# A second fold of the feature transform, with even and odd frequencies apart, and squares added on VectorE ahead of the norm's products

## The chip, the cores and the metric

The kernel runs on one core of a Trainium2 chip. The metric is device time in microseconds (us) of one execution; lower is better. The engines of the core that appear below are TensorE (PE; its weight loads are listed apart as PEld), VectorE (DVE), ScalarE (ACT), GpSimd (POOL) and SyncE (SP), which issues most DMA transfers. Every engine works through its own queue in order, and semaphores make an instruction wait for work of another engine.

## What is computed

The inputs are float32: q, k, v of shape (4, 8, 1152, 64) and two weight matrices, 512x2048 and 2048x512. The reference, cut to what matters:

```python
q_pool = q.reshape(B, H, S // 2, 2, D).mean(axis=3)          # 576 queries of 1152
scores = np.matmul(q_pool, k.transpose(0, 1, 3, 2)) / np.sqrt(D)
attn = softmax(scores)
x = np.matmul(attn, v)              # then heads side by side: x is (4, 576, 512)

X = np.fft.fft(np.fft.fft(x, axis=1), axis=2)
u = x + np.real(X)
un = (u - mean(u)) / np.sqrt(var(u) + 1e-06)                 # over the 512 features
ch = np.maximum(un @ w_ch1, 0.0) @ w_ch2
out = u + ch
```

The real part of the two-dimensional transform is cos over features times cos over tokens, less sin times sin. Below it is called the DFT, the mean and variance the norm, and the two products with w_ch1 and w_ch2 the FFN.

## The kernel before

**Attention.** Work goes by units: a unit is a pair of heads and one block of 128 queries, 5 units to a pair, 80 in all. In a unit TensorE makes the scores (L209, two float32r products to a piece of 384 keys), VectorE takes them out of PSUM with a running minimum (L211), ScalarE takes the exponential (L223), TensorE transposes (L236), ScalarE and in one case of five VectorE copy the transposed tiles to SBUF (L239), and TensorE multiplies with v (L252). When a batch's 8 heads are done, its x stands in two tiles, `ua` and `ub`, [128, 2, 576] each, with features on partitions.

**The middle of a batch** (`mid`: `dft`, then `norm`). `ub` holds features 256 to 511 in mirrored order (the heads' order HEADS, and the mirrored columns of v, see to most of that), so that feature n of `ua` lies beside 512-n of `ub`; a few one-row copies (L418 to L424) put right the rows that don't fit. Then sums and differences `xs` (L431) fold the features once, L445 folds the tokens, and the transform over features is a product with a contraction over 256 features, two tiles of 128 (L454): 256 sine columns, 258 cosine columns. A product with a contraction over a single row (L452, constant `alt`) brings in feature 256. The token transform is L462. `norm` sums the features with a product with `onesm` (L494), subtracts the mean, squares on ScalarE (L503), sums the squares with 24 products of one column each (L510, an [128, 96] block of squares as weights each time), and spreads 1/sqrt(var) with L527.

**What a float32 product is.** In the trace each float32 product of these stages stands as two matmul instructions with a weight load each: the 24 products of L510 are 48.

**FFN.** A block is 12 products of 288 columns (L615 to L617, three to a tile). The first layer's block ends with a Relu on ScalarE (L633) and a remainder on VectorE (L634), the second's with an addition on VectorE (L645). There are 64 blocks to a batch.

**What sets the order.** One program text emits all of it, in an order that a planner writes out: it keeps a clock `now`, adds the cost each step yields, and lets `mid` steps run when they are due and FFN blocks when TensorE credit has come up. A step of `mid` yields (TensorE cost, delay until the next step may be emitted); `gap` is 600 ns for the first three batches and 0 for the last one. The engines then run what they were given in that order, whatever time it really takes. Batch 3's `mid` runs after the last attention unit, beside the remaining FFN blocks of batch 2. Conversions of the weights (L559 to L577, on ScalarE, VectorE and GpSimd) run beside the attention of batches 0 to 2.

## Time and profile before

| | |
|---|---|
| time, median of 3 runs | 1076.02 us (1073.26 to 1076.13) |
| profiled execution, span of its instructions | 1075.9 us |
| TensorE matmul busy | 1015.1 us, 94% |
| TensorE weight load busy | 935.1 us, 87% |
| VectorE busy | 597.9 us, 56% |
| ScalarE busy | 529.4 us, 49% |
| GpSimd busy | 366.1 us, 34% |
| mean granted TensorE clock | 0.974 |

The profile shows no total of the profiled execution apart from its span; the span lies 0.1 us under the median of the runs. The busy share is an average over stages with different limits. Matmuls overlap one another in the records, so the time that a row of matmuls takes is read from the start of the first to the start of what follows. The granted clock is the share of TensorE's full speed (2.4 GHz) that it was given; 0.5 is its lower level, 1.2 GHz.

### The profile page before, as it was taken

To read this page: it belongs to the slowest core of one execution; us is meant where nothing else is said; L and a number is where in the kernel's file an instruction comes from. 1 tells how busy PE (TensorE), PEld (TensorE's weight loads), DVE (VectorE), ACT (ScalarE), POOL (GpSimd) and SP (SyncE) were. 2 spreads that over 40 slices of the span, in tenths; PEclk is the share of its full clock that TensorE was granted. 3 is DMA by queue.
4 is the path that set the end of the run, shared out by engine and by line. 5 is a ranking of instruction groups with operands and counts; after the bars stand their busy time and mean duration, and the time that the engine had idled before them with its cause. 6 is when DMAs were issued, how large, how long until landed. Compare 5 with 4: busy or idle time off the path is not lost.

```text
span 1075.9 us, 22038 instructions
## 1 busy us (share of the span) xinstructions
PE 1015.1 (94%) x8688; PEld 935.1 (87%) x8688; DVE 597.9 (56%) x1542; ACT 529.4 (49%) x1045; POOL 366.1 (34%) x351
## 2 busy tenths in 40 slices
PE   6999998998999989996699999999999999999998
PEld 5898887687999876896599998789999997999998
DVE  5556868877575676665535455654464433442222
ACT  5778876677565665464245454454454431221111
POOL 3545665757455556435322222320220002000000
PEclk9999999989999999998799999999999999899999
DMA  5545644655667653745634433333533242356554
GB/s 181 178 133 173 201 155 166 194 160 186 201 216 245 217 175 106 226 139 182 210 99 165 148 130 118 98 109 131 163 106 113 79 141 70 115 173 198 163 166 153
DMA packets 53709, 168.97 MB, mean 157 GB/s; under 512 B 8083, under 2 KB 11300, under 8 KB 53606
## 3 DMA queue, kind: packets, MB, share of 16 engines
q1 hardware_dynamic: 49286, 149.87, 43.2%
q0 software_dynamic: 4320, 17.70, 5.1%
q8 instruction: 68, 1.11, 0.4%
q14 instruction: 35, 0.29, 0.1%
HBM read 145.97 MB, written 21.57 MB: 156 GB/s over the span
## 4 chain that ended last, share of the span: by engine, by line
PE 70%; DVE 8%; issue 3%; POOL 3%; DMA 2%; ACT 2%; SPq 0%; DVEq 0%; POOLq 0%; ACTq 0%
PE s L209 9%; PE o L252 9%; PE f L615 9%; PE f L616 8%; PE f L617 8%; PE t L236 8%; PE t L615 4%; PE t L617 4%; PE t L616 4%; DVE sp L211 2%; PE f L462 2%; PE f L510 1%; PE f L454 1%; DMA w<-wraw 1%; ACT sp L223 1%
## 5 line engine op out<-in xcount | busy, mean ns | idle before, releaser
L211 DVE TENSOR_SCALAR_CACHE_REDUCE sp<-s,bia 128x384 f32<-128x384 f32 x288 | 177.4, 616 | 98.0 <-PE s L209 77.6
L209 PE MATMUL s<-ks,qh 128*128 128x384 f32 x480 | 185.2, 386 | 26.0 <-DVE sp L211 8.6
L239 ACT COPY pt<-t 128x512 f32<-128x512 f32 (+2 forms) x243 | 126.0, 529 | 126.4 <-PE t L236 122.5
L223 ACT ACTIVATE sp<-sp,bia 128x1152 f32<-128x1152 f32 x144 | 180.0, 1255 | 1.8 <-DVE sp L211 1.7
L252 PE MATMUL o<-pt,vs 128*64 128x128 f32 (+1 forms) x2880 | 167.7, 269 | 3.4 <-DVE pt L239 2.9
L252 PEld LDWEIGHTS o<-pt,vs 128*64 128x64 f32 x2880 | 147.8, 139 | 24.9 <-issue 19.0
L209 PE MATMUL s<-ks,ql 128*128 128x384 f32 x480 | 165.5, 345 | 0.0
L236 PE MATMUL t<-ident,sp 128*128 128x128 f32 x1045 | 152.5, 278 | 1.7 <-ACT sp L223 0.7
L236 PEld LDWEIGHTS t<-ident,sp 128*128 128x128 f32 x1045 | 124.6, 142 | 13.8 <-issue 4.1
L209 PEld LDWEIGHTS s<-ks,qh 128*128 128x128 f32 x480 | 93.1, 194 | 34.0 <-DVE sp L211 11.4
L615 PE MATMUL f<-unh,w 128*128 128x288 f32 x348 | 107.5, 309 | 5.0 <-DVE g L634 5.0
L615 PE MATMUL f<-g,w 128*128 128x288 f32 x348 | 108.0, 310 | 3.1 <-DVE x L645 1.4
L616 PE MATMUL f<-unh,w 128*128 128x288 f32 x348 | 103.9, 299 | 0.0
L617 PE MATMUL f<-unl,w 128*128 128x288 f32 x348 | 103.7, 298 | 0.0
L616 PE MATMUL f<-g,w 128*128 128x288 f32 x348 | 103.7, 298 | 0.0
L617 PE MATMUL f<-g,w 128*128 128x288 f32 x348 | 103.5, 297 | 0.0
L634 DVE SCALAR_TENSOR_TENSOR g<-f,g 128x288 fp32r<-128x288 f32 x87 | 39.7, 457 | 106.7 <-ACT g L633 106.5
L645 DVE TENSOR_TENSOR x<-f,x 128x288 f32<-128x288 f32 x87 | 39.7, 456 | 104.2 <-PE f L617 104.2
L209 PEld LDWEIGHTS s<-ks,ql 128*128 128x128 f32 x480 | 93.5, 195 | 0.6 <-POOL ql L158 0.4
L179 POOL TENSOR_TENSOR ks<-kr,ks 64x1152 fp32r<-64x1152 f32 x30 | 80.6, 2685 | 32.8 <-issue 16.5
L575 POOL TENSOR_TENSOR rest<-rest,wt 128x512 f32<-128x512 f32 x32 | 42.4, 1326 | 143.0 <-DVE wt L570 97.8
L633 ACT ACTIVATE g<-f 128x288 fp32r<-128x288 f32 x87 | 35.4, 410 | 103.5 <-PE f L617 103.4
(129 smaller groups left out, 2015.5 us busy)
## 6 DMA issues: line engine op xcount, KB each, us to landing
w<-w SPq DMA_DIRECT2D x128, 512.0 KB
qr<-in_q SPq DMA_DIRECT2D x30, 576.0 KB
ks<-in_k POOLq DMA_DIRECT2D x30, 576.0 KB, 5.6
wraw<-in_w SPq DMA_DIRECT2D x32, 512.0 KB
w<-wraw SPq DMA_DIRECT2D x32, 512.0 KB
vs<-in_v SPq DMA_DIRECT2D x32, 288.0 KB
kr<-in_k SPq DMA_DIRECT2D x30, 288.0 KB
out<-x SPq DMA_DIRECT2D x12, 288.0 KB
```

The costliest lines, as they stand in the source:

```text
L179: nc.gpsimd.tensor_tensor(ks[D:, :], kr[D:, :], ks[D:, :].bitcast(F32), op=ALU.subtract)
L209: nc.tensor.matmul(ps, lhsT=l, rhs=k, start=i == 0, stop=i == len(ops) - 1)
L211: nc.vector.tensor_scalar(sp[n, j][:, c], ps, -0.0625, bt[:, pc - 1:pc] if pc else None, op0=ALU.mult, op1=ALU.min, accum_out=bt[:, pc:pc ...
L223: last_exp[0] = nc.scalar.activation(t, t, AF.Exp, bias=bia.pop((n, j))[:, 2:3], scale=-1.0, accum_out=den[pr][:, col:col + 1]).ins
L236: nc.tensor.transpose(ps[:, i * P:i * P + P], sp[k][:, c * P:(c + 1) * P], ident)
L239: (nc.vector.tensor_copy if eng == "v" else nc.scalar.copy)(pt[:, :o], ps[:, :o])
L252: nc.tensor.matmul(po[y * D:y * D + D, :w], lhsT=qkv[2 * pr + y][3][:, c, :], rhs=pt[:, o:o + w], start=c == 0, stop=c == NKC - 1)
L575: nc.gpsimd.tensor_tensor(rest, rest, t[:, 0, :], op=ALU.mult)
L615: nc.tensor.matmul(ps, lhsT=ah, rhs=bh, start=first, stop=False)
L616: nc.tensor.matmul(ps, lhsT=al, rhs=bh, start=False, stop=False)
L617: nc.tensor.matmul(ps, lhsT=ah, rhs=bl, start=False, stop=last)
L634: after(1000, lambda: nc.vector.scalar_tensor_tensor(g[:, 1, c], ps[:, :HT], 0.0, g[:, 0, c].bitcast(F32), op0=ALU.max, op1=ALU.subtract))
```

## The change

The DFT folds the features a second time: feature n lies beside 256-n as well. The rows of the two tiles are ordered for that on the host (UROW, HEADS, MIRRORED). After the fold, even frequencies need a+c or a-c, odd ones the other, so that each product has one contraction over 128 rows and half as many frequencies: per block of 96 or 97 tokens two products of 128 columns (sine), or three of 65, 64 and 128 columns (cosine), in place of two of 256, or one single-row product and two of 258. The constant `alt` goes. VectorE and ScalarE get the second fold (`fold`) and other one-row copies, in smaller pieces with a planner's delay between them. In `norm`, VectorE adds the four blocks of squares to one, and 6 products are left of 24. The costs that `dft` and `norm` tell the planner are halved where products are (900 to 450, 2000 to 1000).

```diff
-        nc.vector.tensor_copy(tmp[D:D + 1], ub[:1])
-        nc.scalar.copy(last, ub[D:D + 1, 1, :])
+        nc.vector.tensor_copy(tmp[D:D + 1, 0, :], ua[:1, 1, :])
+        nc.scalar.copy(last, ub[:1, 1, :])
         yield 0, gap
-        nc.vector.tensor_copy(ub[:1, 1, :], ub[D:D + 1, 0, :])
+        nc.vector.tensor_copy(tmp[D:D + 1, 1, :], ub[:1, 0, :])
+        nc.scalar.copy(ua[:1, 1, :], ua[D:D + 1, 1, :])
+        yield 0, gap
         nc.vector.tensor_copy(ub[:1, 0, :], last)
-        yield 0, 1500
-        nc.scalar.copy(ub[D:D + 1], tmp[D:D + 1])
-        yield 0, 1800
+        nc.scalar.copy(ub[:1, 1, :], ub[D:D + 1, 0, :])
+        yield 0, gap
+        nc.vector.tensor_copy(ua[D:D + 1, 1, :], tmp[D:D + 1, 0, :])
+        yield 0, gap
+        nc.scalar.copy(ub[D:D + 1, 0, :], tmp[D:D + 1, 1, :])
+        yield 0, 1200
...
+        def fold(y):
...
+            for j in range(2):
+                nc.vector.tensor_tensor(e[:, j, 1:HT], e[:, j, 1:HT], e[:, j, NH:], op=ops[y])
+                yield 0, gap
+            if y:
+                nc.vector.tensor_tensor(o, a, c, op=ALU.subtract)
+                yield 0, gap
+                nc.vector.tensor_tensor(a, a, c, op=ALU.add)
+                yield 0, gap
+                nc.vector.tensor_copy(a[:1], c[:1])
+                sets.extend(((a, SSETS[0], slice(0, P)), (o, SSETS[1], slice(P, 2 * P))))
+                yield 0, 2500 if gap else 4500
+            else:
+                nc.vector.tensor_tensor(o, a, c, op=ALU.subtract)
+                yield 0, gap
+                nc.vector.tensor_tensor(c, a, c, op=ALU.add)
+                yield 0, gap
+                nc.scalar.copy(a, c)
+                yield 0, 800
+                nc.vector.tensor_copy(c[:1], o[:1])
+                nc.scalar.copy(o[:1], z)
+                sets.extend(((a, CSETS[0], slice(0, 65)), (c, CSETS[1], slice(65, 129)), (o, CSETS[2], slice(129, 257))))
+                yield 0, 1500
...
-                if y == 0:
-                    nc.tensor.matmul(ps[:m, :n], lhsT=z[:, c], rhs=alt, start=True, stop=False)
-                for j in range(2):
-                    nc.tensor.matmul(ps[:m, :n], lhsT=e[:, j, c], rhs=c1[:, j, :], start=y == 1 and j == 0, stop=j == 1)
+                for e, o, i in sets:
+                    nc.tensor.matmul(ps[:m, o], lhsT=e[:, c], rhs=c1[:, 0, i], start=True, stop=True)
                 nc.scalar.copy(yy[:m, t, :], ps[:m, :n])
-                yield 900, 0 if t < 2 else 1200 if y or not gap else 3000
+                yield 450, 0 if t < 2 else 1200 if y or not gap else 3000
...
+        for sq in sqs:
+            nc.vector.tensor_tensor(sq[:, :2], sq[:, :2], sq[:, 2:], op=ALU.add)
+            yield 0, gap
+            nc.vector.tensor_tensor(sq[:, 0], sq[:, 0], sq[:, 1], op=ALU.add)
+            yield 0, 900
         ps = gtile()
         for t, sq in enumerate(sqs):
             for i in range(3):
-                for j in range(4):
-                    nc.tensor.matmul(ps[:96, 3 * t + i:3 * t + i + 1], lhsT=sq[:, j, i * 96:i * 96 + 96], rhs=onesm[:, :1],
-                                     start=j == 0, stop=j == 3)
-        yield 2000, 0
+                nc.tensor.matmul(ps[:96, 3 * t + i:3 * t + i + 1], lhsT=sq[:, 0, i * 96:i * 96 + 96], rhs=onesm[:, :1],
+                                 start=True, stop=True)
+        yield 1000, 0
```

The order of the instructions moves in three places that matter here. The line numbers of the changed kernel are its own: its L423 to L434 are the one-row copies, L441 the first fold, L456 to L474 the token fold and the second feature fold, L488 the transform over features, L541 and L543 the additions of squares, L548 the sum of squares; L672 is before's L634, L683 before's L645, L292 before's L287.

VectorE, batch 3's `mid` after the last attention unit. Before:

```order
L634 SCALAR_TENSOR_TENSOR g<-f,g 128x288 [waits Activation_49] x2
L418 COPY tmp<-x 1x1152 [waits DVE_49,Pool_49]
L421 COPY x<-x 1x576 [waits DVE_49]
L422 COPY x<-last 1x576 [waits Activation_49]
L634 SCALAR_TENSOR_TENSOR g<-t,g 128x288 [waits Activation_49]
L645 TENSOR_TENSOR x<-t,x 128x288 [waits PE_49] x2
L431 TENSOR_TENSOR xs_10630<-x 128x576 [waits DVE_49,Activation_49]
L431 TENSOR_TENSOR xs_10630<-x 128x576
L431 TENSOR_TENSOR xs_10633<-x 128x576 x2
```

The same place in the changed kernel (z is a one-row sum, xs_10581 the differences, xs_10584 the sums):

```order
L672 SCALAR_TENSOR_TENSOR g<-t,g 128x288 [waits Activation_49]
L441 TENSOR_TENSOR xs_10581<-x 128x576 [waits DVE_49] x2
L441 TENSOR_TENSOR xs_10584<-x 128x576 x2
L447 TENSOR_TENSOR z<-xs_10581 1x287 [waits DVE_49]
L448 COPY z<-xs_10581 1x2
L456 TENSOR_TENSOR xs_10581<-xs_10581 128x287 [waits DVE_49]
L456 TENSOR_TENSOR xs_10581<-xs_10581 128x287
L459 TENSOR_TENSOR bs<-xs_10581 128x289 [waits DVE_49]
L461 TENSOR_TENSOR xs_10581<-xs_10581 128x289 [waits DVE_49]
L463 COPY xs_10581<-xs_10581 1x289 [waits DVE_49]
L672 SCALAR_TENSOR_TENSOR g<-t,g 128x288 [waits Activation_49]
L683 TENSOR_TENSOR x<-t,x 128x288 [waits PE_49] x3
```

There are eight remainders (L634, then L672) after the last attention unit in each kernel. Before, the eighth stands ahead of the first fold; in the changed kernel it stands behind the first fold, the token fold and the second fold of the differences.

TensorE, the same batch: the end of the FFN block ahead of the sine transform, the transform, and the block behind it. Before, two FFN blocks more stand ahead of it:

```order
L615 MATMUL f<-g,w_10600 128x288
L616 MATMUL f<-g,w_10600 128x288
L617 MATMUL f<-g,w_10600 128x288
L454 MATMUL f<-cs_109,xs_10633 97x256 [waits DVE_49] x2
L454 MATMUL t<-cs_109,xs_10633 96x256 x4
```

In the changed kernel:

```order
L653 MATMUL t<-g,w_10518 128x288 [waits Activation_49]
L654 MATMUL t<-g,w_10518 128x288
L655 MATMUL t<-g,w_10518 128x288 [waits DVE_49]
L488 MATMUL t<-cs_109,xs_10581 97x128
L488 MATMUL t<-cs_109,bs 97x128
L488 MATMUL f<-cs_109,xs_10581 96x128
L488 MATMUL f<-cs_109,bs 96x128
```

Between the transpose of the reciprocals (L265, the last product of the attention) and the sine transform there are 13 FFN blocks before, 8 of the first layer and 5 of the second. There are 11 in the changed kernel: one of the second layer, 8 of the first, 2 of the second. The wait of L655 is for the eighth L672.

TensorE, the sum of squares of batch 3. Before:

```order
L510 MATMUL t<-onesm,sq 96x1 x12
L510 MATMUL t<-onesm,sq 96x1 [waits Activation_49]
L510 MATMUL t<-onesm,sq 96x1 x11
```

In the changed kernel:

```order
L548 MATMUL t<-onesm,sq 96x1 [waits DVE_49,PE_49]
L548 MATMUL t<-onesm,sq 96x1 x2
L548 MATMUL t<-onesm,sq 96x1 [waits DVE_49]
L548 MATMUL t<-onesm,sq 96x1 x2
```

It waits for VectorE where it waited for ScalarE. In batch 0 the longer chain of delays also moves the first FFN block: before, it stands behind the 32nd unit's product with v, in the changed kernel behind the 34th's. At the 50th unit both kernels emit all that is left of batch 0's FFN, since a tile of x is needed again.

## Rows read from the trace of the kernel before

**Rows 1.** The page, part 1: engine, busy us, share of the span, instructions.

```profile
PE 1015.1 (94%) x8688; PEld 935.1 (87%) x8688; DVE 597.9 (56%) x1542; ACT 529.4 (49%) x1045; POOL 366.1 (34%) x351
```

**Rows 2.** The page, part 4: shares of the chain that ended last, by engine.

```profile
PE 70%; DVE 8%; issue 3%; POOL 3%; DMA 2%; ACT 2%; SPq 0%; DVEq 0%; POOLq 0%; ACTq 0%
```

**Rows 3.** Windows (stretch, busy us by engine, PEclk, DMA) over batches 0, 1, 2.

```profile
160.00:260.00 100.00, 90.67 (x774) 75.00 (x772) 84.11 (x195) 68.69 (x132) 61.88 (x56) 0.95 0.50 164
360.00:460.00 100.00, 89.15 (x744) 76.63 (x743) 69.96 (x164) 59.14 (x114) 59.85 (x54) 0.97 0.54 170
640.00:720.00 80.00, 77.20 (x649) 67.42 (x646) 48.19 (x123) 39.72 (x76) 25.98 (x28) 0.98 0.36 111
```

**Rows 4.** Timeline (start, us, what) of TensorE, batch 3: FFN, transforms, sum of squares.

```profile
882.11 0.30 PE L615 MATMUL t<-g,w 128*128 128x288 f32 x1
...
890.05 1.02 PE L454 MATMUL f<-cs,xs 128*97 128x256 f32 x4
...
892.45 0.48 PE L615 MATMUL t<-g,w 128*128 128x288 f32 x1
...
898.84 0.67 PE L452 MATMUL f<-alt,bs 1*97 1x258 f32 x2
...
903.49 0.48 PE L615 MATMUL t<-g,w 128*128 128x288 f32 x1
...
925.47 5.61 PE L510 MATMUL t<-onesm,sq 128*96 128x1 f32 x48
930.94 0.59 PE L615 MATMUL t<-g,w 128*128 128x288 f32 x1
```

**Rows 5.** Windows around that sum of squares; the clock follows POOL.

```profile
926.00:928.00 2.00, 2.00 (x25) 2.00 (x25) 0.13 (x1) 0.00 (x0) 0.00 (x0) 0.97 0.31 125
928.00:930.00 2.00, 2.00 (x15) 2.00 (x14) 0.00 (x0) 0.00 (x0) 0.00 (x0) 0.50 0.00 0
...
934.00:936.00 2.00, 2.00 (x14) 2.00 (x14) 0.46 (x1) 0.00 (x0) 0.00 (x0) 0.83 0.34 92
```

**Rows 6.** Timeline of TensorE: ten 128-column transposes at full clock.

```profile
461.66 1.25 PE L236 MATMUL t<-ident,sp 128*128 128x128 f32 x10
462.67 0.38 PE L615 MATMUL f<-g,w 128*128 128x288 f32 x1
```

**Rows 7.** Groups by line on VectorE: busy, mean ns of one | idle before.

```profile
L431 DVE TENSOR_TENSOR xs<-x 128x576 f32<-128x576 f32 x16 | 16.0, 1023 | 0.0
L445 DVE TENSOR_TENSOR xs<-xs 128x287 f32<-128x287 f32 x16 | 8.3, 530 | 0.0
L485 DVE TENSOR_TENSOR lsum<-x 128x576 f32<-128x576 f32 x8 | 9.2, 1160 | 0.0
```

**Rows 8.** Timeline, batch 0: first fold on VectorE, GpSimd beside it.

```profile
170.17 4.76 DVE L431 TENSOR_TENSOR xs<-x 128x576 f32<-128x576 f32 x2
...
171.26 3.05 POOL L179 TENSOR_TENSOR ks<-kr,ks 64x1152 fp32r<-64x1152 f32 x1
```

**Rows 9.** Timeline of VectorE, batch 3 after the last attention unit.

```profile
878.32 0.75 DVE L287 TENSOR_TENSOR x<-x,r 128x576 f32<-128x576 f32 x1
...
881.15 0.46 DVE L634 SCALAR_TENSOR_TENSOR g<-f,g 128x288 fp32r<-128x288 f32 x1 [1.14 <-ACT g L633]
...
882.42 0.45 DVE L421 COPY x<-x 1x576 f32<-1x576 f32 x1
...
883.28 0.44 DVE L634 SCALAR_TENSOR_TENSOR g<-t,g 128x288 fp32r<-128x288 f32 x1
...
885.86 2.75 DVE L431 TENSOR_TENSOR xs<-x 128x576 f32<-128x576 f32 x4
...
888.97 0.81 DVE L445 TENSOR_TENSOR xs<-xs 128x287 f32<-128x287 f32 x2
```

**Rows 10.** TensorE behind a stall: its timeline, and a window behind it.

```profile
500.53 0.61 PE L615 MATMUL f<-unh,w 128*128 128x288 f32 x1 [4.97 <-DVE g L634]
...
502.00:504.00 2.00, 2.00 (x10) 2.00 (x9) 1.82 (x5) 0.49 (x1) 0.00 (x0) 0.50 0.62 197
```

More of the change, by code (lines that the diff above doesn't have):

```diff
@@ L432, in dft @@
                 yield 0, gap
-            xs.append(e)
+            xs.insert(0, e)
         bs = mtile([P, 3, NH], F32, "bs")
-        z = bs[:1, 2, :]
-        nc.vector.tensor_tensor(z[:, 1:HT], last[:, 1:HT], last[:, NH:], op=ALU.add)
-        nc.vector.tensor_copy(z[:, 0:NH:HT], last[:, 0:NH:HT])
-        for y, n in ((1, 256), (0, 258)):
+        x1 = xs[1][:1, 0, :]
+        nc.vector.tensor_tensor(z[:, 1:HT], x1[:, 1:HT], x1[:, NH:], op=ALU.add)
+        nc.vector.tensor_copy(z[:, 0:NH:HT], x1[:, 0:NH:HT])
+        def fold(y):
+            e = xs[y]
+            ops = ALU.add, ALU.subtract
+            a, c, o = e[:, 0, :NH], e[:, 1, :NH], bs[:, 2, :]
+            for j in range(2):
[20 more added lines that the diff above has]
+                yield 0, 1500
+        for y, n in ((1, 256), (0, 257)):
             c1, c2 = ((cc1, cc2), (cs1, cs2))[y]
-            e = xs[y]
-            for j in range(2):
-                nc.vector.tensor_tensor(e[:, j, 1:HT], e[:, j, 1:HT], e[:, j, NH:], op=(ALU.add, ALU.subtract)[y])
-                yield 0, gap if j == 0 else 1500 if y == 0 else 2500 if gap else 4500
+            sets = []
+            yield from fold(y)
             yy = mtile([97, 3, n], F32, f"y{y}")
@@ L450, in dft @@
                 c = slice(t0, t0 + m)
-                if y == 0:
-                    nc.tensor.matmul(ps[:m, :n], lhsT=z[:, c], rhs=alt, start=True, stop=False)
-                for j in range(2):
-                    nc.tensor.matmul(ps[:m, :n], lhsT=e[:, j, c], rhs=c1[:, j, :], start=y == 1 and j == 0, stop=j == 1)
+                for e, o, i in sets:
+                    nc.tensor.matmul(ps[:m, o], lhsT=e[:, c], rhs=c1[:, 0, i], start=True, stop=True)
                 nc.scalar.copy(yy[:m, t, :], ps[:m, :n])
-                yield 900, 0 if t < 2 else 1200 if y or not gap else 3000
+                yield 450, 0 if t < 2 else 1200 if y or not gap else 3000
             for j in range(3 - y):
@@ L780, in _constants @@
 def _constants():
-    n = np.arange(DM // 2)
-    a1 = 2 * np.pi * (np.outer(n, np.arange(257)) % DM) / DM
+    a1 = 2 * np.pi * (np.outer(np.arange(P), FREQ) % DM) / DM
+    c1 = np.cos(a1)
+    s1 = np.sin(a1)
+    s1[0] = np.sin(np.pi / 2 * (FREQ % 4))
+    s1[0, ::2] = 0.0
     n1 = np.arange(NH)
     a2 = 2 * np.pi * (np.outer(n1, n1) % SQ) / SQ
-    c1 = np.zeros((DM // 2, 258))
-    c1[:, :257] = np.cos(a1)
-    s1 = np.sin(a1[:, :256])
-    s1[:, 0] = 0.0
+    c1 = np.concatenate([c1[:, x] for x in CSETS], axis=1)
+    s1 = np.concatenate([s1[:, x] for x in SSETS], axis=1)
     c2 = np.cos(a2)
@@ L795, in _constants @@
     for i, m in enumerate((c1, s1)):
-        t = m.reshape(2, P, -1).transpose(1, 0, 2).reshape(P, -1)
-        out[i, :, :t.shape[1]] = t
+        out[i, :, :m.shape[1]] = m
     for i, m in enumerate((c2, s2)):
@@ L804, in _constants @@
     out[4, :, P:2 * P] = 1.0 / DM
-    out[4, 0, 2 * P + 1:2 * P + 257:2] = -2.0
     return out
@@ L817 @@
     vt = v.copy()
-    vt[:, H // 2:] = v[:, H // 2:][..., VCOL]
+    vt[:, MIRRORED] = v[:, MIRRORED][..., VCOL]
     v2 = vt.reshape(B, H, NKC, P, D).transpose(0, 1, 3, 2, 4)
```

17 lines of the change are left out of this document (10 added, 7 removed).

## The prediction

> **What bounds the kernel now.** I read the engines' shares first: TensorE is busy 94% of the span, no other engine over 56% [rows 1], and the chain that ended last runs through TensorE for 70% and through VectorE for 8% [rows 2]. So time taken off TensorE counts wherever TensorE is what others wait for. The windows over the middle of each batch show how far that holds there. In 160 to 260 us (batch 0) TensorE is busy 90.7 of 100 us and VectorE 84.1; in 360 to 460 us (batch 1) they are at 89.2 and 70.0; in 640 to 720 us (batch 2) at 77.2 and 48.2 of 80 [rows 3]. TensorE is near full in all three, but in batch 0 VectorE is nearly as full, and the change loads VectorE. Batch 3 runs after the attention, where TensorE alone is full.
>
> **What TensorE saves, per batch.** The sine transform takes from 890.05 to 892.45, 2.40 us for 12 instructions, 0.200 each; the cosine transform from 898.84 to 903.49, 4.65 us for 18 [rows 4]: 7.05 us. After the change there are again 12 and 18 instructions, but with 128 columns at most. Their price stands in no row, so it is bounded. Low end: ten 128-column transposes took 1.01 us, 0.101 each [rows 6]. High end: the 0.200 of 256 columns [rows 4], if half the columns brought nothing. Nearest is the sum of squares: a float32 product with a weight load of 96 columns and one column to stream, 48 in 925.47 to 930.94, 0.114 each [rows 4]; since even one column costs that, the load sets the pace, and I take 0.115. Thirty instructions are 3.45 us; saved 3.6 us (4.0 at the low end, 1.05 at the high end).
>
> The Trainium skill ("TensorE: Matmul & The Clock Gate", section Back-to-back issue gap) gives a sustained pace of about 81 ns for a load and a product of 128 columns; an estimate by it is 30 x 0.081 = 2.4 us, a saving of 4.6 us per batch. The 0.114 us of one column [rows 4] is above it, so here the row decides.
>
> The sum of squares: 48 instructions in 5.47 us become 12, 1.37 us at the same pace; saved 4.1 us. The products are of the same shape, so there is no other end.
>
> The clock: about 3 us into the sum of squares the granted clock drops to 0.50, its lower level, and is back only in the window from 934 [rows 5]. The FFN products behind it start at 930.94 [rows 4] and pay for it: some 3.7 us at half clock is about 1.8 us lost, and I take 1.65. All four batches have the 48 instructions. With a quarter of the instructions I expect no drop; the other end is that it still drops, 0 saved.
>
> Sum per batch: 3.6 + 4.1 + 1.65 = 9.35 us, 37.4 us for four. With the low price of each unknown at its worst it is 1.05 + 4.1 = 5.15, 20.6 us for four.
>
> **What VectorE and ScalarE get, per batch.** VectorE: four two-input operations of 289 columns, like the token fold at 0.53 each [rows 7], 2.1 us; two one-row copies of 289, about 0.45 each by the 0.45 of a 576-column one [rows 9], 0.9; in the norm two additions of 576 columns at 1.16 and two of 288 at 0.53 [rows 7], 3.4. The one-row copies ahead come out nearly even (four of 576 for one of 1152 and two of 576), with some 0.6 for four starts in place of three. Together 7.0 us. ScalarE gets one copy of 289 columns, one one-row copy and two more starts, under 2 us. SyncE loses one small load, GpSimd is as before.
>
> The other end of VectorE's price: with GpSimd at work, the first fold took 4.76 us for two operations [rows 8], where batch 3, with GpSimd idle, took 2.75 for four [rows 9]: 2.38 against 0.69. If all eight new two-input operations met that, they would cost 19 us and the whole 20.5. The mean of the same line, 1.02 [rows 7], says that most don't; I stay with 7.0. The lower end, 0, is that VectorE has room for all.
>
> How much reaches the end in batches 0 to 2: the score products wait for L211 on VectorE, which stands in the same queue, so I charge the added 7.0 us by VectorE's busy share there. Batch 0: 7.0 x 0.84 = 5.9, and the FFN starts two units later, about 16 us more without FFN to fill TensorE's gaps (the 32 units before the first FFN block end about where the first window of rows 3 does, 260 / 32 = 8.1 us each), at 9.3 idle in 100 [rows 3], 1.5: gain 9.35 - 5.9 - 1.5 = 2.0. Batch 1: 9.35 - 7.0 x 0.70 = 4.45. Batch 2: 9.35 - 7.0 x 0.60 = 5.15. New waits lie in this charge: VectorE's one-row copy (L473) now waits for a ScalarE copy emitted 0.8 us before it, with L211 behind it in the queue, and the cosine products wait for ScalarE's last one-row copy.
>
> **Batch 3.** Here the delays are 0 and the order decides. Before, the eighth remainder (883.28) ran ahead of the first fold (885.86 to 888.6), and TensorE came from the FFN to the sine transform at 890.05, just as the token fold (888.97, 0.81) was done [rows 4, 9]: no idle time. In the changed order the eighth remainder stands behind the first fold, the token fold and the second fold, and the second of the two FFN blocks ahead of the transform needs it for its last product. TensorE: five blocks took 882.11 to 890.05 [rows 4], 1.59 each. The eight blocks of the first layer end one block later than the 882.11 of before, at 883.7; one block more is 885.3, and 11 products of the next 886.75. VectorE: the sixth remainder now takes the place at 881.15; four one-row copies on ScalarE and VectorE at 0.45 to 0.7 each, a Relu and the seventh remainder follow, so the first fold starts at about 885.0. Then 2.75 for it, 0.5 for z, 0.81 for the token fold, 3 x 0.42 for the second fold and the row copy, 0.46 for the remainder: 890.75. TensorE waits about 3.9 us where it did not wait. After a wait of 4.97 us the clock stood at 0.50 for the products that follow 500.53 [rows 10], some 3.9 us, 1.7 lost to those 16 products; I take 1.7 here too. The additions of squares cost 0.3 more, since the second pair ends just after TensorE comes to them. Gain 9.35 - 3.9 - 1.7 - 0.3 = 3.45 us.
>
> **Sum.** 2.0 + 4.45 + 5.15 + 3.45 = 15.05 us off the profiled 1075.9 us is 1060.85; with the 0.1 that the median lies above the span, 1061.
>
> **Rivals.**
> *All of TensorE's time comes back.* VectorE has room (60 to 84% busy [rows 3]) and the charge for it falls away: 37.4 less 1.5 less the 5.9 of batch 3 is 30.0, 1046; without the wait in batch 3, 1040. For it: TensorE is at 94% [rows 1]. Against it: VectorE's 84% in batch 0.
>
> *It does less than it says.* Halved columns bring 1.05 in place of 3.6, and the clock falls as before: 10.2 and 6.6 less than the sum; with one of them about 1071 or 1068, with both 1078, no gain. For it: the load, not the columns, sets the pace of short products [rows 4].
>
> *VectorE's collisions with GpSimd make it slower.* The place is the middle of batches 0 to 2, where GpSimd works beside the added two-input operations; a charge above 9.35 us to a batch turns each into a loss, and above some 10 us the whole is slower, since batch 3 keeps 3.45 and the late FFN costs 1.5. At 13 us each: 3 x 3.65 + 1.5 - 3.45 = 9.0 us, 1085; with all eight at 2.38 in each batch, 1107. For it: rows 8. Against it: the mean in rows 7.
> The Trainium skill ("SBUF — State Buffer", section Who interferes with whom) states the rule behind this: a VectorE instruction with two SBUF inputs contends with a GpSimd instruction that reads SBUF, and the one that issues second waits for the other. The trace agrees in the 2.38 us.
>
> **How the numbers follow.** Chances: the forecast 0.55, its own range 1052 to 1070; all of it comes back 0.22 (1038 to 1052); less than it says 0.12 (1068 to 1079); slower by collisions 0.11 (1077 to 1107). A measurement of this kernel can tell about 0.3% from no change, 1072.8 to 1079.2. Faster than that: 0.54 + 0.22 + 0.05 = 0.81; within it: 0.01 + 0.07 = 0.08; slower: 0.11. The range leaves out the top of the second and third rivals and the bottom of the first: 1042 to 1074.
>
> **What would show it.** Right: 30 short products of the transform in about 3.5 us; 12 instructions of the sum of squares in 1.4 us with the clock at 1.00 behind them; TensorE idle for some 4 us ahead of the sine transform of batch 3, ended by the remainder (L672), and half clock behind it; VectorE's busy time up by 20 to 30 us. Wrong: TensorE's busy time down by less than 20 us; TensorE's waits for L211 up by more than 10 us in the middle of batches 0 to 2; a changed stall at the 50th unit, where both kernels emit what is left of batch 0's FFN, which I count at nothing because both do it.

## The result, and the profile after

The changed kernel takes 1085.84 us (median of 4 runs, 1084.02 to 1088.8), the kernel before 1075.02 us: 1.0097 times as long, 95% interval 1.0073 to 1.0122. Forecast were 1061 us and a range of 1042 to 1074. The profiled execution spans 1085.0 us at a mean granted clock of 0.966. Times below are medians too; one of the four runs of e7 (1116.4 us, at a clock of 0.84) is left out of its median.

Part 1 of its page, and its windows over the stretches of [rows 3]:

```profile
PE 997.8 (92%) x8544; PEld 924.4 (85%) x8544; DVE 624.3 (58%) x1586; ACT 531.0 (49%) x1061; POOL 368.6 (34%) x351
```
```profile
160.00:260.00 100.00, 81.21 (x694) 67.61 (x689) 79.49 (x180) 61.58 (x123) 56.91 (x53) 0.91 0.46 146
360.00:460.00 100.00, 89.61 (x758) 81.11 (x756) 76.30 (x178) 57.49 (x116) 53.68 (x47) 0.97 0.55 180
640.00:720.00 80.00, 78.54 (x704) 71.88 (x703) 52.66 (x136) 42.46 (x88) 26.90 (x26) 1.00 0.39 122
```

TensorE is busy 17.3 us less than in [rows 1], but the span grew by 9.1, so TensorE is idle for 87.2 us where it was 60.8. The first window says where: batch 0, with 9.5 us less busy time and the clock at 0.91 against 0.95 [rows 3]. Batch 2 (third window) has its clock at 1.00.

**Where along the run.** Both kernels compute the same 80 units, so the traces can be laid side by side: the end of a unit's last product with v after, less the same end before, less 1.6 us (1.59 by [rows 4]) for each FFN block that one kernel has done more. The change stands at -4.0 us after unit 25, +20.2 after unit 40, +16.1 after unit 50, +21.3 after unit 52 (behind the drain: at the 50th unit the FFN blocks of batch 0 up to the 60th of its 64 are emitted at once; in both kernels the last four come later), +20.7 after unit 60, +13.6 after unit 70, +9.0 at the end. So batches 2 and 3 won some 12 us; batch 0 and the drain lost more.

Between the ends of units 20 and 50 TensorE is idle for 42.3 us (21.5 before) and 37.5 us run at half clock (17.0 before), which loses half of them. That is 20.8 + 10.2 = 31 us of loss against some 17 us of products saved by then (the transforms and sums of squares of batches 0 and 1, at 4.1 and 4.2 us each by the rows of batch 3 below).

**One of the stalls, batch 0.** TensorE, ScalarE, VectorE and GpSimd in turn, and the window behind the stall (qr and ks are the next heads' tiles, wt, rest and wraw those of a weight conversion):

```profile
197.74 2.19 PE L257 MATMUL o<-pt,vs 128*64 128x128 f32 x36
...
215.52 0.90 PE L488 MATMUL f<-cc,xs 128*96 128x65 f32 x4 [5.32 <-ACT y L489]
...
216.84 3.77 PE L257 MATMUL o<-pt,vs 128*64 128x128 f32 x36
```
```profile
205.20 0.67 ACT L189 CAST qh<-qr 128x576 fp32r<-128x576 f32 x1 [4.45 <-POOL qr L183]
...
206.26 0.43 ACT L471 COPY xs<-xs 128x289 f32<-128x289 f32 x1
...
211.81 0.67 ACT L597 ACTIVATE wt<-wraw 128x512 f32<-128x512 f32 x1 [2.83 <-POOL wraw L615]
...
212.63 1.25 ACT L228 ACTIVATE sp<-sp,bia 128x1152 f32<-128x1152 f32 x1
...
213.88 1.24 ACT L228 ACTIVATE sp<-sp,bia 128x1152 f32<-128x1152 f32 x1
...
215.12 0.62 ACT L489 COPY y<-f 97x257 f32<-97x257 f32 x2
```
```profile
206.72 1.31 DVE L473 COPY xs<-bs 1x289 f32<-1x289 f32 x1 [2.50 <-ACT xs L471]
```
```profile
203.77 1.40 POOL L183 TENSOR_TENSOR qr<-qr 128x576 f32<-128x576 f32 x1
...
207.95 1.26 POOL L613 TENSOR_TENSOR rest<-rest,wt 128x512 f32<-128x512 f32 x1
...
210.51 1.26 POOL L615 TENSOR_TENSOR wraw<-wt,rest 128x512 fp32r<-128x512 f32 x1
```
```profile
216.00:220.00 4.00, 4.00 (x35) 3.72 (x36) 0.00 (x0) 0.37 (x1) 0.00 (x0) 0.50 1.01 284
```

ScalarE waits 4.45 us for GpSimd's L183, then 2.83 us for the conversion's L615. Behind these waits stand two copies that have nothing to do with either: L471, for which VectorE waits, and L489, for which TensorE waits 5.32 us. Between L597 and L489 ScalarE also has 2.5 us of exponentials of the attention (L228) to do, so about half of the 5.32 us are the conversion's. After that the clock is at 0.50, and the same 36 products that took 2.19 us take 3.77.

TensorE's waits (line, waited for: us in all, times, longest):

```profile
PE f L653 <- DVE g L672: 10.8, 6, 3.8
PE s L214 <- ACT pt L244: 8.6, 6, 5.7
PE o L257 <- DVE pt L244: 7.4, 3, 3.7
...
PE f L488 <- ACT y L489: 5.9, 2, 5.3
...
PE t L655 <- DVE g L672: 3.7, 1, 3.7
```

No single wait makes up the loss. The last is the one forecast for batch 3.

### The profile page after: what moved, and what is told of

It reads as the page before. It is cut to its first block, busy times and chain, and to the rows that moved or that the text cites. A ratio compares the mean times of both kernels' runs of the same rounds, so it can differ in the third digit from the quotient of the medians.

```text
span 1085.0 us, 21808 instructions
## 1 busy us (share of the span) xinstructions
PE 997.8 (92%) x8544; PEld 924.4 (85%) x8544; DVE 624.3 (58%) x1586; ACT 531.0 (49%) x1061; POOL 368.6 (34%) x351
## 3 DMA queue, kind: packets, MB, share of 16 engines
q1 hardware_dynamic: 49284, 149.60, 42.8%
## 5 line engine op out<-in xcount | busy, mean ns | idle before, releaser
L216 DVE TENSOR_SCALAR_CACHE_REDUCE sp<-s,bia 128x384 f32<-128x384 f32 x288 | 177.4, 616 | 107.1 <-PE s L214 86.5
L214 PE MATMUL s<-ks,qh 128*128 128x384 f32 x480 | 187.1, 390 | 20.2 <-ACT pt L244 8.6
L228 ACT ACTIVATE sp<-sp,bia 128x1152 f32<-128x1152 f32 x144 | 180.1, 1255 | 0.1
L257 PEld LDWEIGHTS o<-pt,vs 128*64 128x64 f32 x2880 | 150.2, 141 | 27.8 <-issue 18.7
L653 PE MATMUL f<-unh,w 128*128 128x288 f32 x352 | 111.4, 317 | 13.8 <-DVE g L672 10.3
L654 PE MATMUL f<-unh,w 128*128 128x288 f32 x352 | 107.0, 304 | 0.0
L655 PE MATMUL f<-unl,w 128*128 128x288 f32 x352 | 106.6, 303 | 0.0
L655 PE MATMUL f<-g,w 128*128 128x288 f32 x344 | 103.0, 299 | 0.0
L672 DVE SCALAR_TENSOR_TENSOR g<-f,g 128x288 fp32r<-128x288 f32 x88 | 40.2, 456 | 105.7 <-ACT g L671 105.5
L683 DVE TENSOR_TENSOR x<-f,x 128x288 f32<-128x288 f32 x86 | 39.2, 456 | 89.5 <-PE f L655 89.3
```

What stands on the lines that cost most here:

```text
L214: nc.tensor.matmul(ps, lhsT=l, rhs=k, start=i == 0, stop=i == len(ops) - 1)
L216: nc.vector.tensor_scalar(sp[n, j][:, c], ps, -0.0625, bt[:, pc - 1:pc] if pc else None, op0=ALU.mult, op1=ALU.min, accum_out=bt[:, pc:pc ...
L228: last_exp[0] = nc.scalar.activation(t, t, AF.Exp, bias=bia.pop((n, j))[:, 2:3], scale=-1.0, accum_out=den[pr][:, col:col + 1]).ins
L257: nc.tensor.matmul(po[y * D:y * D + D, :w], lhsT=qkv[2 * pr + y][3][:, c, :], rhs=pt[:, o:o + w], start=c == 0, stop=c == NKC - 1)
L653: nc.tensor.matmul(ps, lhsT=ah, rhs=bh, start=first, stop=False)
L654: nc.tensor.matmul(ps, lhsT=al, rhs=bh, start=False, stop=False)
```

## The experiments

**The theories.** A: the costs and delays that the change tells the planner move every later instruction of batches 0 and 1 to another place in the in-order queues, and the loss is that order (a later FFN start and a longer drain first of all). B: the loss is the new work, on VectorE above all. C: the conversions' chain over ScalarE, VectorE and GpSimd sets the pace of batches 0 and 1, and what stands behind it waits.

All runs in one table. "Ratio" is to the kernel before, with its interval. The other columns are the side-by-side differences in us after a unit, from the one profiled execution (which can lie up to 5 us from the median).

| | us | ratio | 25 | 40 | 50 | 52 | 70 | end |
|---|---|---|---|---|---|---|---|---|
| changed kernel | 1085.8 | 1.0097 [1.0073, 1.0122] | -4.0 | 20.2 | 16.1 | 21.3 | 13.6 | 9.0 |
| e1 | 1089.6 | 1.0122 [1.0102, 1.0141] | -3.7 | 10.8 | 8.0 | 10.9 | 11.1 | 12.1 |
| e2 | 1079.4 | 1.0039 [1.0026, 1.0052] | -1.7 | 16.7 | 6.6 | 16.6 | 7.1 | 3.1 |
| e3 | 1075.3 | 0.9985 [0.9964, 1.0006] | -0.2 | 1.0 | 1.1 | 7.8 | 0.9 | -2.2 |
| e4 | 1084.6 | 1.0084 [1.0060, 1.0108] | -6.9 | 17.5 | 13.3 | 17.2 | 10.8 | 9.8 |
| e5 | 1077.3 | 1.0019 [1.0002, 1.0036] | -0.5 | 5.2 | 7.6 | 6.0 | 3.4 | 0.2 |
| e6 | 1082.7 | 1.0072 [1.0046, 1.0098] | -4.3 | 20.0 | 16.1 | 21.1 | 11.0 | 2.8 |
| e7 | 1039.0 | 0.9672 [0.9642, 0.9702] | -10.2 | -16.0 | -26.0 | -36.0 | -38.8 | -40.0 |
| e8 | 1031.8 | 0.9594 [0.9568, 0.9621] | -16.3 | -10.2 | -31.7 | -33.3 | -42.8 | -44.3 |
| e9 | 1064.3 | 0.9895 [0.9873, 0.9918] | -0.2 | -0.2 | -0.2 | -1.6 | -8.7 | -13.3 |
| e10 | 1083.8 | 1.0084 [1.0069, 1.0099] | 0.2 | 3.0 | -0.7 | 6.1 | 3.9 | 5.9 |
| e11 | 1087.5 | 1.0118 [1.0086, 1.0150] | -4.2 | 17.1 | 15.8 | 22.6 | 12.0 | 7.3 |
| e12 | 1066.2 | 0.9919 [0.9902, 0.9936] | -1.5 | 4.6 | 2.0 | 3.5 | -6.6 | -14.1 |
| e13 | 1074.9 | 0.9994 [0.9972, 1.0015] | -4.3 | 15.8 | 10.6 | 15.8 | 4.5 | 0.5 |
| e14 | 1077.6 | 1.0032 [1.0014, 1.0049] | -2.8 | 14.7 | 13.0 | 18.7 | 10.1 | 4.8 |
| e15 | 1075.5 | 1.0001 [0.9989, 1.0013] | -2.4 | 6.3 | 11.1 | 14.9 | 4.4 | -2.4 |
| e16 | 1075.9 | 1.0006 [0.9989, 1.0023] | -2.4 | 8.3 | 6.0 | 11.7 | 1.8 | -5.5 |
| e17 | 1087.8 | 1.0124 [1.0088, 1.0159] | 6.1 | 11.1 | 9.7 | 10.9 | 9.3 | 8.3 |
| e18 | 1081.9 | 1.0062 [1.0039, 1.0084] | -0.4 | 1.6 | 0.4 | 5.0 | 3.9 | 3.2 |

### Order without work: e1 and e2

e1 is the kernel before with only longer delays, so that its FFN starts a unit later; e2 is the changed kernel with shorter ones, so that it starts at unit 32 again.

Both edits stand in `dft` and in `norm`; e1:

```diff
-        gap = 600 if b < B - 1 else 0
+        gap = 940 if b < B - 1 else 0
```

e2:

```diff
-        gap = 600 if b < B - 1 else 0
+        gap = 380 if b < B - 1 else 0
```

> The kernel before, with the planner's delay between the small steps of batches 0 to 2 raised from 600 to 940 ns and nothing else: the same operations, but the first FFN block stands behind the 33rd unit in place of the 32nd, and batch 0's middle is about as long as in the changed kernel. Theory A (the later FFN leaves TensorE unfilled while batch 0's middle runs, and that is where the time went): 6 to 14 us slower than before, with TensorE idle 8 us or more beyond before's between units 25 and 40. Theory B (the loss is made by the new instructions: ScalarE copies that VectorE waits for, and more VectorE work): within 3 us of before.

> The changed kernel, with the delay between its small steps cut from 600 to 380 ns in batches 0 to 2, which makes the middle's delays as long in sum as before's; the first FFN block stands behind the 32nd unit again. Theory A: the loss of batch 0 goes, 1060 to 1068 us, with units 20 to 40 not slower than before. Theory B: the new waits are all there, closer together; 1078 us or more.

A delay that adds no instruction costs the kernel before 14 us; a shorter one gives the changed kernel 6 back. Order alone can make a loss of this size: e1 came at the top of theory A's range. e2 did not come as A had it (1060 to 1068): its 1079.4 lies where B had it, so the FFN's start is at most a part of the loss.

### The two parts apart: e3, e4, e5

e3 is the kernel before with the norm's part alone (the last hunk of the diff above), e4 the changed kernel without that hunk. e5 has the norm's part, but its additions are put straight behind the squares, with no delay of their own and the old cost, so that everything else keeps its place (`add_up` makes the two additions of the diff above):

```diff
+            if sqs:
+                add_up(sqs[0])
             sqs.append(sq)
             yield 0, 1800
+        add_up(sqs[1])
...
         yield 2000, 0
```

> The kernel before with the change to the norm alone: VectorE adds the squares, 12 instructions on TensorE in place of 48 for the sum of squares. The prediction's terms: 4.1 us of TensorE and 1.65 us of clock per batch, against 3.4 us of VectorE's work per batch; charged by VectorE's busy share, about 13 us faster, 1060 to 1066. Theory A: the delays grow by 3 us in sum and the FFN starts where it did, so nothing is lost in batch 0: 1058 to 1066. Theory B (VectorE's added work costs what it saves): 1070 to 1078.

> The changed kernel with the norm of before: the second fold alone, first FFN block behind the 34th unit. Theory A: the loss of batch 0 is in here nearly whole, 1083 to 1095 us. Theory B, if it is the second fold's waits: the same, 1083 to 1095; if it is the norm's VectorE work: below 1080. The clock falls behind the 48 instructions of the sum of squares again, in each batch.

> The norm's change alone, as in e3, but with the planner told the same costs and delays as before, so that every other instruction keeps its place: the first pair of additions stands behind the second square, the second pair just ahead of the products. Theory A (the saving is real, and what ate it in batches 0 and 1 is the shifted order): 1056 to 1066 us, every batch faster by 3 to 6 us. Theory B (the instructions themselves, VectorE's additions ahead of waiting products, eat it in batches 0 and 1): 1068 to 1076, with batches 2 and 3 alone some 11 us faster.

The norm's part costs nothing, where A had named a gain and B none, and the transform's costs 9 us, as both had it. In e3 batches 2 and 3 save 6.9 and 3.1 us (unit 52 to 70, 70 to the end), but the drain takes 6.7 us more. e5 lies 1 us above B's range and far above A's: it keeps every other instruction in its place, and still stands 7.6 us behind after unit 50, with the products saved. It shows the other price: products right behind VectorE's additions make TensorE wait for these (L503 in its numbering) where it did not wait before:

```profile
PE f L516 <- DVE sq L503: 13.7, 6, 4.6
```

### Named suspects: e6, e11, e7, e8

e6 puts batch 3's eighth remainder ahead of the fold again. e11 moves two copies of the cosine fold from ScalarE to VectorE, L471 of the stall among them. e7 and e8 are the kernel before and the changed one without the weight conversions.

e6, ahead of the first fold:

```diff
-        yield 0, 1200
+        yield 0, 1200 if gap else 2800
```

e11, in `fold`:

```diff
-                nc.scalar.copy(a, c)
+                nc.vector.tensor_copy(a, c)
...
-                nc.scalar.copy(o[:1], z)
+                nc.vector.tensor_copy(o[:1], z)
```

e7 and e8, in `convert`, take parts of k in place of the weights and leave out the conversion's arithmetic on all three engines:

```diff
-        nc.sync.dma_start(w, src[f].bitcast(I32).rearrange("p (c x) -> p c x", x=2))
+        nc.sync.dma_start(w, k2[f // 4 % 4, f % 8, :, :1024].bitcast(I32).rearrange("p (c x) -> p c x", x=2))
```

> The changed kernel with one delay raised from 1200 to 2800 ns in batch 3 alone, so that the eighth remainder stands ahead of the first fold again. By the trace of after, TensorE's idle time ahead of the sine transform (3.7 us) and half the 3.4 us at half clock go: 4 to 6 us faster than after, 1080 to 1082. If the stall is made by the longer fold itself and not by the place of the remainder: within 2 us of after.

> The changed kernel with the two ScalarE copies inside the cosine fold (L471, L474) moved to VectorE, nothing else moved in the planner's order. It takes away VectorE's wait for ScalarE there (L473, 2.50 us in batch 0) and the position of the copy behind ScalarE's own wait for GpSimd. Theory C (ScalarE's queue behind GpSimd's conversions, handed on to VectorE through this copy): 2 to 5 us shorter, 1081 to 1084 us; the 5.3 us wait of L488 for the y copy stays, since that copy stays on ScalarE. Theory A (only the places in the order count): same as the changed kernel, within 2 us of 1085.

> The kernel before without the arithmetic of the weight conversion: the ten operations on ScalarE, VectorE and GpSimd are left out, and the weights' place is taken by parts of k of the same size, loaded and stored by the same DMAs at the same places of the order. It is there for the comparison with e8. TensorE's idle time in batches 0 and 1 falls in any case; 1035 to 1065 us.

> The changed kernel without the arithmetic of the weight conversion, as e7. Theory C (in batches 0 and 1 the queues of ScalarE, VectorE and GpSimd, held by the conversions and by what waits behind them, set the pace, so TensorE's saving is not seen there): without the conversions the saving arrives, 18 to 32 us faster than e7. Theory A (the shifted order and the later FFN cost it, with or without conversions): less than 10 us faster than e7, or slower.

e6 gave 3 us of the 4 to 6 expected, with intervals that overlap: the 3.7 us wait of L655 is gone, and the sine transform waits 2.0 us for the fold (L463) instead. e11 gave nothing, which was theory A's reading: VectorE's wait for L471 went, and TensorE's came in its place:

```profile
PE f L488 <- DVE xs L471: 4.2, 1, 4.2
```

Without conversions the kernel before takes 1039.0 us and the changed one 1031.8: 0.7% shorter, where with them it is 1.0% longer. So 18.0 us of the change's place (from -7.2 to +10.8) hang on the conversions. But theory C had named 18 to 32 us between e7 and e8 and A less than 10: the 7.2 us are A's reading, and of some 33 us that the products save in four batches (8.3 each by the rows of batch 3 below) most stays lost without conversions too. Leaving them out also takes four operations of each off VectorE, so the pair does not tell waits for conversions (C) from a full VectorE (B). Without them the changed kernel still loses 12 us between units 25 and 40 against the kernel before (-6.1 to +5.8), of which it gets 11.5 back by unit 50; the drain then takes 8.4.

### Where it pays: e9 and e10

The kernel before with the norm's part in batches 2 and 3 alone (e9), and in batches 0 and 1 alone (e10). The edit of e9 in `norm` (e10 has `b >= 2` there):

```diff
+        if b < 2:
...
+            yield 2000, 0
+        else:
+            for sq in sqs:
+                nc.vector.tensor_tensor(sq[:, :2], sq[:, :2], sq[:, 2:], op=ALU.add)
...
+            yield 1000, 0
```

> The kernel before with the norm's edit in batches 2 and 3 alone; batches 0 and 1 keep the 48 one-column products and, with them, the order of before instruction by instruction (FFN from unit 32, 50 blocks by the 50th unit). Theory A/C (the loss is made in batches 0 and 1, where the order settles how conversions and folds share the queues, and in the drain at the 50th unit that follows from it): nothing is lost up to the 52nd unit, and batches 2 and 3 keep what they gave in the norm alone (6.9 us in batch 2, 3.1 in the tail): 1075 - 10 = 1065 us, ratio 0.991, with TensorE's summed waits no longer than before's 61 us. Theory B (VectorE's six further instructions take back what the products give, wherever they stand): batches 2 and 3 pay too, 1073 to 1077.

> The complement: the norm's edit in batches 0 and 1 alone. Theory A/C: the products saved there (4.1 us each) do not reach the end, the FFN has 48 blocks instead of 50 by the 50th unit, and the drain after it is longer: +6 to +8 us at the 52nd unit, 1081 to 1083 us; together with the run for batches 2 and 3 the differences add up to the norm's alone (-1 us). Theory B: what VectorE's additions cost is spread over all batches, so this run lies within 2 us of the kernel before.

e9 came as theory A and C had it, e10 0.8 us above their range. The same edit gives 10.7 us in batches 2 and 3 and costs 8.8 in batches 0 and 1; e9 is 1.0% faster than the kernel before. In e9 every column up to unit 50 is -0.2, and the 6.8 us at half clock behind batch 3's sum of squares are gone. VectorE's additions do not lose time wherever they stand (theory B as e9 tests it). That they lose it in batches 0 and 1, where VectorE is fullest, these two runs do not exclude; e16 below bears on that.

### The changed work in another order: e12 to e16

e12 has the whole change. Its planner's numbers were chosen by the FFN's start (unit 32) and the blocks done by unit 50 (48); e6's and e11's edits are in it.

```diff
-    RATES = [0.0, 1.12, 0.97, 0.97, 0.97]
+    RATES = [0.0, 1.25, 0.97, 0.97, 0.97]
...
-        gap = 600 if b < B - 1 else 0
+        gap = 380 if b < B - 1 else 0
...
-                yield 450, 0 if t < 2 else 1200 if y or not gap else 3000
+                yield 900, 0 if t < 2 else 1200 if y or not gap else 3000
...
-        yield 1000, 0
+        yield 2000, 0
...
-        yield 7000
+        yield 5500
...
-            cdue = now + (10000 if nb == 0 else 8500)
+            cdue = now + (10000 if nb == 0 else 8000)
```

> The changed kernel with its work kept and the planner's numbers set so that the FFN starts at unit 32 as before (34 in the changed kernel) and has 48 blocks by the 50th unit (46): the products' costs back at 900 and 2000 ns, gap 380, conversions told shorter (5500, due after 8000), FFN rate of batch 1 at 1.25; in batch 3 the fold waits 2800 for the remaining eighth; the two copies of the cosine fold on VectorE. Theory A (the late FFN start and the 14-block drain carry most of the loss): 1070 to 1076 us, drain idle about 5 us smaller. Theory C (the folds' own place among the conversions carries it): 1076 to 1081 us, since the folds of batches 0 and 1 still stand among the conversions. Theory B: no better than 1080.

It came out at 1066.2, better than any theory had said: 19.6 us under the changed kernel with the same arithmetic, 0.8% under the kernel before. The same place of batch 0 in e12, ScalarE and then TensorE:

```profile
204.53 0.67 ACT L189 CAST qh<-qr 128x576 fp32r<-128x576 f32 x1 [3.15 <-POOL qr L183]
205.11 0.37 ACT L489 COPY y<-f 97x257 f32<-97x257 f32 x1
205.37 0.67 ACT L597 ACTIVATE wt<-wraw 128x512 f32<-128x512 f32 x1
```
```profile
205.53 0.55 PE L488 MATMUL f<-cc,xs 128*96 128x65 f32 x4 [2.66 <-ACT y L489]
```

The y copy stands ahead of L597, and that one finds its conversion done. TensorE waits 2.66 us in place of 5.32, now behind the cast's wait for GpSimd. The windows between units 20 and 35 of the changed kernel and of e12, and the same stretch of e13 (below), whose unit 35 ends at 292:

```profile
146.00:296.00 150.00, 125.89 (x1084) 106.78 (x1084) 118.28 (x279) 98.97 (x196) 85.73 (x76) 0.92 0.48 154
```
```profile
146.00:299.00 153.00, 131.89 (x1176) 113.83 (x1176) 123.31 (x291) 101.64 (x200) 87.47 (x79) 0.98 0.55 174
```
```profile
146.00:299.00 153.00, 127.18 (x1106) 108.52 (x1107) 118.84 (x288) 99.99 (x198) 85.11 (x76) 0.92 0.53 162
```

The clock is 0.98 in e12 and 0.92 in the others. Between units 20 and 50 e12 has 17.0 us at half clock, as many as the kernel before, and 34.9 us idle.

Which of its numbers did it? e13, e14 and e15 each take one back (the gap; the products' costs; the conversions' numbers and the rate), e16 the norm's part in batches 0 and 1.

> The re-planned version with the gap back at 600: the FFN starts at unit 34 again and has 3 blocks by the 35th unit (11 in the re-planned), but 48 by the 50th as there. If the late FFN start carries the loss (TensorE has nothing that could fill the waits of batch 0's transform): 1074 to 1080 us. If the blocks done by the 50th unit and the conversions' places carry it: 1066 to 1069 us.

> The re-planned version with the change's own costs of 450 and 1000 ns for the products; FFN start at 32 and 48 blocks by the 50th unit stay. If the FFN's start and lead carry the loss: 1064 to 1069 us, no difference. If it is the planner's clock, which runs ahead less by these costs and so brings conversions and copies to other places: 1071 to 1078 us.

> The re-planned version with the conversions' numbers and the FFN rate as in the changed kernel (told 7000, due after 8500, rate 1.12); costs 900 and 2000, gap 380, FFN start at 32 and 48 blocks by the 50th unit stay. If the FFN's start and lead carry the loss: 1064 to 1069 us. If the places of the conversions among GpSimd's and ScalarE's work carry it (the waits behind which L189's cast and L489's copy stood): 1073 to 1080 us.

> The re-planned version with the old norm in batches 0 and 1. If the norm's edit loses in batches 0 and 1 by what VectorE does there: 4 to 8 us shorter, 1058 to 1062 us. If it lost there by the order alone, which the new plan has mended: 2 to 6 us longer, since 4.1 us of products a batch come back: 1068 to 1072 us.

e13, e14 and e15 came where the number taken back was to carry the loss, e16 above both of its ranges. Each loses 9 to 11 us, and not in one place: e13 and e14 between units 25 and 40, e15 between 40 and 45, e16 between 25 and 35, and all four in the drain as well (3.8 to 5.7 us against 1.5 in e12, with 12 blocks in all five). FFN start at 32 and 48 blocks by unit 50 hold in e14 and e15 too. So theory A in its narrow form, the FFN's start and lead, fell: they are not enough. e16 is 9.7 us longer than e12, so under this plan VectorE's additions in batches 0 and 1 bring a gain, where they cost 8.8 us in e10. The 9.7 are not the price of the norm's part alone, since taking it out moves the order as well.

### The same numbers for the kernel before: e17 and e18

e17 has e12's gap, conversion numbers and rate on the kernel before, e18 the conversion numbers and the rate alone.

> The kernel before, its work unchanged, with the planner's numbers of the re-planned version: gap 380, conversions told 5500 and due after 8000, FFN rate of batch 1 at 1.25 (the products' costs were 900 and 2000 already). If the numbers are better for any kernel: 1062 to 1068 us. If the order suits only the work it was found for: 1073 to 1085 us, as with the other orders tried that moved the middle of batches 0 and 1.

> The kernel before with the conversions' numbers alone (told 5500, due after 8000, rate 1.25), gap 600 as it was. Same reading: 1062 to 1070 us if the earlier conversions are a gain by themselves; 1073 to 1083 us if every move of them against the folds costs.

They cost it 12 and 6 us, e17 beyond the range given for a loss. So e12's numbers are no better in themselves. All three other orders tried for the work of before (e1, e17, e18) are slower than its own by 6 to 14 us; seven other orders for the changed work, five of them with e11's copies on VectorE, lie between 1066 and 1087 us.

**What is settled and what is not.** Shown: the loss does not lie in the new work as such, since the same arithmetic under another plan is 8.8 us faster than the kernel before (e12); it is made in batches 0 and 1 and the drain (the table, e9, e10), where an order without new work costs as much (e1); and e12's numbers suit the changed work and not that of before (e17, e18). It is not shown that the work costs nothing in any order: in the order of before the norm's part gave no gain (e5). With the conversions out of the queues the change gains, but little (e7, e8). Open: which neighbours in the queues decide, since each number moved hundreds of instructions, and the loss came back at a different place each time. A second buffer for the conversions, against the wait of L597, was not tried.

## Why the prediction was wrong, point by point

**What TensorE saves: right in the sum, by a price that was misread.** The rows of batch 3, first the stall ahead of the sine transform, then the cosine transform and the sum of squares, each with what follows it:

```profile
902.87 0.61 PE L655 MATMUL t<-g,w 128*128 128x288 f32 x1 [3.71 <-DVE g L672]
903.27 0.63 PE L488 MATMUL t<-cs,xs 128*97 128x128 f32 x2
...
905.68 0.59 PE L653 MATMUL t<-g,w 128*128 128x288 f32 x1
...
913.70 0.47 PE L488 MATMUL f<-cc,xs 128*97 128x65 f32 x4
...
915.29 0.38 PE L653 MATMUL t<-g,w 128*128 128x288 f32 x1
...
940.36 1.40 PE L548 MATMUL t<-onesm,sq 128*96 128x1 f32 x12
941.62 0.38 PE L653 MATMUL f<-g,w 128*128 128x288 f32 x1
```

The 18 instructions of the cosine transform take 1.59 us, 0.088 each, at full clock. The 12 of the sine transform behind the stall take 2.41 at half clock; in e12, at full clock, 1.31, 0.109 each. That is 2.9 us for 30, against 3.45 taken and 7.05 before [rows 4]. The estimate of 2.4 us by the pace in the Trainium skill ("TensorE: Matmul & The Clock Gate", section Back-to-back issue gap) is too low for these 30. The sum of squares takes 1.26 us, against 1.37, with a pause of 0.3 us for the second pair of additions.

The 0.114 that set the price was no price at full clock: its row ran at half clock from 928 us on [rows 5]. Batch 2 of the kernel before (clock 1.00 in 704 to 708 us) and batch 1 of the changed one show one-column instructions at full clock, 48 in 4.10 us and 12 in 0.96:

```profile
704.17 4.24 PE L510 MATMUL f<-onesm,sq 128*96 128x1 f32 x48
708.27 0.63 PE L236 MATMUL t<-ident,sp 128*128 128x128 f32 x4
```
```profile
465.58 1.10 PE L548 MATMUL f<-onesm,sq 128*96 128x1 f32 x12
466.54 0.63 PE L241 MATMUL t<-ident,sp 128*128 128x128 f32 x4
```

So one column costs 0.080 to 0.085 us and 128 cost 0.109: that 0.115 lay close was luck. TensorE's busy time fell by 17.3 us, less than the 20 that the prediction had named as a sign of being wrong: more of it ran at half clock (0.966 in the mean, 0.974 before).

**The clock term: right in batches 1 and 3, the wrong way round in the sum.** Behind the 12 instructions of batch 3 it stays at full speed, behind the stall it does not:

```profile
902.00:904.00 2.00, 1.13 (x5) 1.13 (x6) 1.60 (x5) 0.00 (x0) 0.00 (x0) 0.70 0.00 0
904.00:906.00 2.00, 2.00 (x11) 2.00 (x10) 0.00 (x0) 0.74 (x2) 0.00 (x0) 0.50 0.65 217
...
942.00:944.00 2.00, 2.00 (x18) 2.00 (x17) 0.46 (x1) 0.20 (x1) 0.00 (x0) 1.00 0.00 0
```

In batches 0 and 2 it falls behind the sum of squares even so (0.57 in 264 to 268 us, 0.58 in 739 to 743): there its second half waited 1.76 and 1.43 us for VectorE's additions. And the 1.65 us were booked as a gain for batches 0 and 1 too, where between units 20 and 50 new waits brought 20.5 us more at half clock: 10.2 us lost in place of 3.3 won.

**What VectorE gets: right.** Its groups for the added operations (busy us, mean ns), of four batches:

```profile
L541 DVE TENSOR_TENSOR sq<-sq 128x576 f32<-128x576 f32 x8 | 8.4, 1049 | 0.0
L543 DVE TENSOR_TENSOR sq<-sq 128x288 f32<-128x288 f32 x8 | 5.9, 738 | 0.1
L461 DVE TENSOR_TENSOR xs<-xs 128x289 f32<-128x289 f32 x4 | 3.7, 936 | 0.0
L467 DVE TENSOR_TENSOR bs<-xs 128x289 f32<-128x289 f32 x4 | 3.2, 800 | 0.1
L469 DVE TENSOR_TENSOR xs<-xs 128x289 f32<-128x289 f32 x4 | 2.6, 646 | 0.1
...
L473 DVE COPY xs<-bs 1x289 f32<-1x289 f32 x4 | 2.3, 579 | 2.5 <-ACT xs L471 2.5
...
L459 DVE TENSOR_TENSOR bs<-xs 128x289 f32<-128x289 f32 x4 | 1.9, 468 | 0.0
```

With L463's 2.3 that is 30.3 us, 7.6 a batch against 7.0, and VectorE's busy time rose by 26.4. The rival in which VectorE collides with GpSimd named 1085 us, the time that came; but its mechanism is not what happened, since the means of these rows are 0.47 to 1.05 us, far from 2.38.

**How much reaches the end in batches 0 to 2: the step that failed.** It charged VectorE's added time by VectorE's busy share, and so took the rest of the order as fixed. Batch 0: +2.0 forecast, but 20.2 us lost by unit 40. The wait that the charge stood for did not grow: TensorE waited 8.6 us for L211 before and 7.4 us for the same line, L216, after (first line before, the others after):

```profile
PE s L209 <- DVE sp L211: 8.6, 7, 1.8
```
```profile
PE t L241 <- DVE sp L216: 4.2, 3, 2.3
...
PE s L214 <- DVE sp L216: 3.2, 5, 1.2
```

What came in its place are waits all over the order (above), most of all for the FFN's remainders, which stand behind other work on VectorE: 20.9 us for L672 in all, 9.2 for L634 before. The text of the change held what the sum left out: it halves the costs told to the planner and adds delays, so that folds, conversions, heads' preparations and FFN blocks all change their neighbours.

**The late FFN, 1.5 us: mis-sized.** e13, which starts it at unit 34 again, is 8.8 us longer than e12, though its gap moves the folds' steps too. The clock belongs to that price: it is 0.92 in e13's window above and 0.98 in e12's.

**The stall at the 50th unit, "counted at nothing because both do it": wrong.** With 46 FFN blocks done by then (50 before), 14 have to come at once and not 10. The windows over it, before, after, in e12 and in e9:

```profile
484.00:542.00 58.00, 40.26 (x277) 36.15 (x272) 29.67 (x66) 23.30 (x47) 28.68 (x25) 0.77 0.59 189
```
```profile
494.00:563.00 69.00, 49.08 (x315) 44.09 (x312) 34.87 (x76) 26.87 (x53) 34.51 (x29) 0.80 0.60 204
```
```profile
483.00:545.00 62.00, 42.89 (x291) 38.93 (x285) 33.27 (x70) 25.08 (x49) 30.72 (x24) 0.83 0.60 202
```
```profile
484.00:540.00 56.00, 38.02 (x270) 34.09 (x266) 30.02 (x66) 22.89 (x44) 26.93 (x25) 0.79 0.60 195
```

The drain is 11 us longer (58 to 69), by the side-by-side differences 5.2 more than four blocks at 1.6 explain: a block costs more there than elsewhere, with the clock at 0.80. Of the 11 us, 8.8 are TensorE's busy time, where four blocks at full clock are 6.4, and 2.2 are idle.

**Batch 1.** From unit 40 to 50 the change wins 4.1 us, near the 4.45 forecast, and the drain takes it back; the nearness may be luck, since e1, which saves no product, wins 2.8 us there. **Batch 2:** 7.1 us won from unit 60 to 70, against 5.15. **Batch 3: right in its mechanism.** The wait for the eighth remainder is 3.71 us (3.9 forecast), half clock behind it; from the last unit to the end the change wins 4.8 us against 3.45. Where the order leaves little to go wrong, counting instructions was enough.

## What to carry to other kernels

In a program whose whole order is written out ahead, an edit's new costs and delays are an edit of their own: compare the order everywhere it moves (what stands behind each wait, how many blocks are done at each forced drain), not only at the instructions that are new. Test such an edit apart from the order, by keeping the order and changing the work, or the other way round, and give the new work an order of its own before judging it. Where that can't be done, apply it first where queues are quiet: here the batches without conversions.
